# Staging rooms, a deferred store, earlier differences and a last product by token rows in a gated mix of linear attention and eight experts

## The chip, the cores and the metric

The kernel runs on one core of one Trainium2 chip. The metric is the device time of one execution in microseconds (us), lower is better. A core has four compute engines that are used here: TensorE (PE in the profile, with its weight loads as PEld), VectorE (DVE), ScalarE (ACT) and GpSimd (POOL). SyncE (SP) only issues DMAs. Each engine runs its own instructions in the order in which they were written; semaphores hold an instruction until what it needs is there. The kernel schedules by hand: the order on each engine is the order in which the Python program calls the operations, and the tile framework adds the waits.

## What is computed

For 2048 tokens of width 512:

```python
x = A_x
g = sigmoid((x * gate_w).sum(-1, keepdims=True))
a = linear_attention(x, wqkv) @ wo        # 32 heads, phi(t) = (t + 1 if t > 0 else exp(t)) + 1e-6
# mixture: K = 8 of 8 experts, so each token passes all of them
w = softmax(x @ w_gate)
b = sum(w[:, e:e+1] * (silu(x @ w1[e]) @ w2[e]) for e in range(8))   # 512 -> 1792 -> 512
out = g * a + (1 - g) * b
```

Nearly all of the arithmetic is the experts' two matrix products. All of it is in float32; each float32 operand is split into a high and a low part, and a product is three matmuls (high by high, high by low, low by high, `mm3`, L57 to L60).

## The kernel before

**Stages.** `keys` (L319) computes keys and values of the attention and the gates' logits. `experts` (L578) then runs one long loop over steps u. In every step there is a piece of an up product (x by w1) and, from step 58 on, a piece of a down product (hidden by w2), called tick n = u - 58. Both products use a seven-product scheme for 2 by 2 blocks (products P1, P7, P2, P4, P6, P5, P3 in this order): sums and differences of blocks are formed on VectorE, and seven products replace eight. The hidden blocks' differences are formed by `difference` (L716), called by `differ` (L727) at fixed numbers of ticks after a part's first product: kind 1, 2 and 3 at 6, 15 and 29 ticks.

**Groups and steps.** A group g is a pair of hidden blocks of one part (one expert for one half of the tokens); it takes seven steps, k = 0 to 6, one product of 6 matmuls of 512 columns each. Groups 0 and 1 are the attention's queries, groups 2 to 8 are the first expert's. In each step `up` (L644) calls, in order: `other()` (the preparation of the next group's weights, the splits of hidden blocks into high and low by `high`, L741, on ScalarE and `low_h`, L758, on VectorE, and the differences), then the up product, then `mid()` (the tick), then the copies out of PSUM. At k = 6 the last of them is the addition at L696 on VectorE, and the product of the next k = 1 accumulates on the same bank, so it waits for that addition.

**Weights.** For the first half of the tokens, the second weight matrix of an expert is also prepared here: `prep` (L190) makes its high parts on ScalarE (`high2`, L212) and its low parts on VectorE (`low2`, L216) in a staging tile, from which `stash` (L184) stores it to a scratch in device memory, by DMAs of SP's queue. Later `load_w2` (L776) brings these back in pairs, in the order of the ticks. The staging tile number i (0 to 3 in each group) is taken by `ws_tile` (L208): i = 0 is used at k = 1 and stored at k = 2, i = 1 is used at k = 1 and stored at k = 3, i = 2 is used at k = 5 and stored at k = 6, i = 3 is used at k = 6 and stored at the next k = 0. Where it lies is set by `m.spare` (L1112): before step 50 tiles 0 to 2 are taken from `ho` (5 buffers), in the steps 50 to 56 from `xs` (2 buffers), and tile 3 always, and after step 56 all tiles, from `ws` (2 buffers). A buffer can be written again when the DMAs that read it have landed. For the first six pairs of the first expert, the P1 piece is not staged: it is made in the room in which the ticks 0 to 5 use it (`first_w2`, L765) and is stored to the scratch as well, at k = 2 of its group (L250).

**The end.** The last part is the attention's output product for the second half of the tokens, with two pairs: 14 ticks, two for each product. Its results are added by `evict` (L818) to the accumulated sums of the experts in SBUF, which lie with output columns on the partitions; `rows` (L1048) and `columns` (L1056) turn them by TensorE transposes, 128 by 128, copy them out of PSUM and store them. The product P3 is added to the sums of the first 256 columns of the last 512 tokens; after it come the transposes of these sums, the copies and the last stores.

**The start.** SP loads x by four DMAs of 512 columns each, ScalarE's queue loads the first weights by four (L397 to L399). ScalarE makes the high part of x, VectorE makes that of the first weight piece, and the first real matmuls (L451) run. Before them nine matmuls on a tile of zeros run (L513 to L515); that tile is cleared by GpSimd (L388).

Of the kernel before, what the change touches and what calls it, by code (L numbers as in the profile page):

```python
# [16 lines left out]
P = 128  # L17
# [121 lines left out]
def weights(m):  # L139
# [2 lines left out]
    m.ORDER = ("P1", "P7", "P2", "P4", "P6", "P5", "P3")  # L142
    raw, ops, ws = {}, {}, {}
    m.ops = ops
    m.spare = None


    def raw_tile(name, dt=F32):
# [41 lines left out]
    def prep(g, step):  # L190
# [15 lines left out]


        def ws_tile(n):  # L208
            w = ws[g, n] = m.spare(f"wx{g}_{n}") if m.spare and n < 3 else o_tile(f"ws{g}_{n}", "ws", 2, D)
            return w  # L210

        def high2(n, src):  # L212
# [19 lines left out]
        if step == 0:  # L232
            ops[g] = [None] * 7
            high(0, r[:, 0, :, 0], (0, 0), (2, HALF))
        elif step == 1:
            low(0, r[:, 0, :, 0])
            o = o_tile(f"o{g}_1", "oh", 2, HALF)
            act_copy(o[:, 0], r[:, 1, 1, 0])
            ops[g][6] = o, 0
            if both and not begin:  # L240
                ws_tile(0)
            if both:
                act_copy(first(0), r[:, 0, 0, 1])
            high2(1, r[:, :, 1, 1] if both else None)
        elif step == 2:
            o = ops[g][6][0]
            v.tensor_sub(o[:, 1], r[:, 1, 1, 0], f32(o[:, 0]))
            if both:
                v.tensor_sub(first(1), r[:, 0, 0, 1], f32(first(0)))
                stash(part, q, "P1", m.first_w2(q) if begin else ws.pop((g, 0))[:, :, :HALF])  # L250
        elif step == 3:
            low2(1, r[:, :, 1, 1] if both else None, "P2", "P4")
            v.tensor_add(block(1, 1), block(1, 0), block(1, 1))
        elif step == 4:
            v.tensor_sub(block(1, 0), block(0, 0), block(1, 0))
            v.tensor_sub(block(0, 0), block(1, 1), block(0, 0))
        elif step == 5:
            high(2, r[:, 1, :, 0], (5, 0), (1, HALF))
            high2(2, r[:, :, 0, 1] if both else None)
            v.tensor_sub(block(0, 1), block(0, 1), block(0, 0))  # L260
        elif step == 6:
            low(5, r[:, 1, :, 0])
            low2(2, r[:, :, 0, 1] if both else None, "P6", "P7")
            high(3, r[:, 0, :, 0], (3, 0), (4, HALF))
            high2(3, r[:, :, 1, 1] if both else None)
        else:
            low(3, r[:, 0, :, 0])
            low2(3, r[:, :, 1, 1] if both else None, "P3", "P5")
# [44 lines left out]
            low(3, r[:, :, 1], "P3", "P5")  # L313

    m.raw_tile, m.load, m.prep, m.load_wp, m.prep_wp = raw_tile, load, prep, load_wp, prep_wp

def keys(m):  # L319
# [68 lines left out]
    nc.gpsimd.memset(f32(zero), 0.0)  # L388


    gw = [att.tile([P, 2048 + 96 * i], F32R, name=f"g{i}")[:, :2 * KT * G[i]] for i in range(2)]
# [2 lines left out]
    x0 = raw[0] = four(room("x0"))  # L394
    r0 = four(m.raw_tile("r0")[:, :KT * G[0]])
    r1 = [hl_tile(f"r1{i}", F32) for i in range(2)]
    for k in range(KT):  # L397
        nc.sync.dma_start(x0[:, k, :], m.xT[0][:, k * TB:(k + 1) * TB])
        nc.scalar.dma_start(r0[:, k, :], m.wk[:, k * G[0]:(k + 1) * G[0]])  # L399
    for i in range(2):  # L400
        at = KT * G[0] + 2 * i * G[1]
        nc.sync.dma_start(r1[i][:, :, :G[1]], m.wk[:, at:at + 2 * G[1]].rearrange("p (k f) -> p k f", k=2))
    x_tiles(0, 0), x_tiles(0, 1)
    for k in range(KT):
        act_copy(xk(0, 0, k), x0[:, k, :])
# [172 lines left out]
def experts(m, misc):  # L578
# [148 lines left out]
    def differ(u):  # L727
        if u % 7 == 1 and 7 < u < NU + 7 and groups[u // 7 - 1][0].e < E:
            t12, t22 = (raw[u // 7 - 1, f, 1] for f in range(2))
            v.tensor_sub(t12, t22, t12)  # L730
        for pairs, offs in ((NPAIR, (None, 6, 15, 29)), (2, (-3, -1, 1, 5))):
            for kind, off in enumerate(offs):
                if off is None or not 0 <= u - LAG - off < END:
                    continue
                part, prod, q = place(u - LAG - off)
                if part.n == pairs and prod == "P1":
                    difference(kind, part, q)

    SRC = {"P1": 0, "P7": 1, "P2": 2, "P4": 2, "P6": 0, "P5": 0, "P3": 3}
# [78 lines left out]
    def evict(part, prod, sub):  # L818
        b = pb[bank_of(part, prod), sub]
        e = f"{part.h}_{part.e}{sub}"  # L820
        if part is m.A[1]:

            if prod == "P1":
                pb["s", sub] = ps_tile(f"s{sub}", "bc"[sub])
                act_copy(pb["s", sub], b)
                return
            r, j = {"P7": (1, 1), "P2": (0, 0), "P4": (1, 0), "P6": (1, 0), "P5": (1, 1), "P3": (0, 1)}[prod]
            s = sums[1, r * 2 + sub, j]
            for c in range(2) if (prod, sub) == ("P3", 1) else (slice(None),):
# [21 lines left out]

    def tick(n):
        part, prod, k = place(n)
        first = prod in ("P1", "P7")
        for q, sub in STEPS[part.n][k]:
            i = n - k + q
            if q == 0 and first:
                pb[BANK[prod], sub] = ps_tile(f"p{n}_{sub}", "dn")
            w = w2s[i // 2][:, i % 2]
            ds = slice(sub * P, (sub + 1) * P)  # L860
            h = hop[i]
            assert not isinstance(h, tuple)
# [190 lines left out]
        nc.sync.dma_start(m.out[(NHT + i) * P:(NHT + i + 1) * P, :], r)  # L1053


    def columns(dt, tag):  # L1056
        ps = ps_tile(f"oc{dt}", tag)
        for tt in range(NTT):
            nc.tensor.matmul(ps[:, tt * P:(tt + 1) * P], sums[1, dt, 1][:, tt * P:(tt + 1) * P], m.ident,
                             start=tt == 0, stop=True, is_transpose=True, skip_group_check=True)  # L1060
        r = r_tile(f"oc{dt}")
        at = (NHT + NTT) * P
        rows = m.out[at:at + TB, dt * P:(dt + 1) * P].rearrange("(t p) d -> p t d", p=P)
        if dt != 1:
            act_copy(r, ps)
            nc.sync.dma_start(rows, r.rearrange("p (t d) -> p t d", d=P))
            return
        for i, (copy, queue) in enumerate(((act_copy, nc.scalar), (v.tensor_copy, nc.sync))):
            c = slice(i * HALF, (i + 1) * HALF)
            copy(r[:, c], ps[:, c])  # L1070
            queue.dma_start(rows[:, 2 * i:2 * i + 2], r[:, c].rearrange("p (t d) -> p t d", d=P))


    AHEAD = {}
# [21 lines left out]
    for u in range(LAG + NTICK):  # L1096
# [134 lines left out]
```

## Time and profile before

| | |
|---|---|
| median of 3 runs | 2350.26 us (2349.44 to 2350.53) |
| the profiled execution, its own time | 2350.77 us |
| its span (first to last instruction) | 2349.1 us |
| time outside the span in that execution | 1.7 us |
| VectorE busy | 1811.9 us (77%) |
| ScalarE busy | 1419.3 us (60%) |
| GpSimd busy | 158.7 us (7%) |
| DMA | 513.23 MB, mean 218 GB/s |

How to read the profile's rows: a row of the timeline has the start in us from the start of the span, the duration in us, the engine, the line of the kernel, the operation, the names of output and inputs, the shapes and the count, and in brackets how long the engine had been idle and what ended that. "SPq" and "ACTq" are the DMA issues of SyncE and ScalarE. A matmul's duration reaches to the modelled end of its pipeline, so that matmuls that follow one another overlap: their pace is the distance of their starts. A row of the waits has who waited for whom, the total in us, how many times, and the longest. A row of the windows has the stretch, its length, the busy time of PE, PEld, DVE, ACT and POOL with the counts, the granted clock of TensorE, the DMA engines' share and GB/s.

### The profile page before, as it was taken

Reading aid. Unit: us, or ns where it says so; the run is one execution under the profiler, and the core shown is the slowest. Engines: PE = TensorE matmul, PEld = TensorE weight load, DVE = VectorE, ACT = ScalarE, POOL = GpSimd, SP = SyncE. Lnnn points to the kernel's source line nnn. Section 1 sums busy time; section 2 is a strip of 40 time slices with the busy share of each in tenths; the row PEclk is TensorE's granted clock in tenths of the full one; section 3 lists DMA queues with packets and bytes.
Section 4 is the critical chain, followed back from the end, with each engine's and each line's share of the span. In section 5 each row is a group of like instructions: output and inputs, shape, how many; then the busy total and the mean of one; then the engine's idle time right before and its main releaser. Section 6 shows DMA issues by size and latency. Waiting matters only on the chain.

```text
span 2349.1 us, 31301 instructions
## 1 busy us (share of the span) xinstructions
PE 2338.4 (100%) x10492; PEld 1935.4 (82%) x10492; DVE 1811.9 (77%) x3102; ACT 1419.3 (60%) x2655; POOL 158.7 (7%) x222
## 2 busy tenths in 40 slices
PE   9999999999999999999999999999999999999999
PEld 8877888888888888888888888888888888888887
DVE  6798888888888888888677768776676777766666
ACT  6686666666666656666555555555565655555553
POOL 2101000000000000000000000000011000000101
PEclk9999999999999999999999999999999999999999
DMA  7898888988889898988845455654556655555566
GB/s 225 239 311 249 264 288 249 278 263 267 268 267 275 256 290 252 271 269 262 287 144 170 152 172 153 182 186 144 163 166 188 182 150 174 162 166 166 165 220 207
DMA packets 299345, 513.23 MB, mean 218 GB/s; under 512 B 24352, under 2 KB 193840, under 8 KB 298800
## 3 DMA queue, kind: packets, MB, share of 16 engines
q1 hardware_dynamic: 274992, 464.10, 59.8%
q0 software_dynamic: 23344, 46.49, 10.8%
q8 instruction: 82, 1.34, 0.2%
q10 hardware_dynamic: 848, 0.66, 0.1%
q14 instruction: 79, 0.65, 0.1%
HBM read 343.43 MB, written 163.52 MB: 216 GB/s over the span
## 4 chain that ended last, share of the span: by engine, by line
PE 97%; DVE 1%; DMA 1%; issue 0%; ACT 0%; POOL 0%; DVEq 0%; ACTq 0%; POOLq 0%
PE p L58 16%; PE p L60 16%; PE p L59 16%; PE a L58 8%; PE a L60 8%; PE a L59 8%; PE c L59 4%; PE c L58 4%; PE c L60 4%; PE b L60 2%; PE b L59 2%; PE b L58 2%; PE g L451 2%; DMA w2stash<-w 1%; PE y L58 1%; PE y L60 1%
## 5 line engine op out<-in xcount | busy, mean ns | idle before, releaser
L58 PE MATMUL p<-ho,w 128*128 128x512 f32 x1620 | 631.4, 390 | 0.8 <-DVE d L844 0.6
L60 PE MATMUL p<-ho,w 128*128 128x512 f32 x1620 | 630.3, 389 | 0.0
L59 PE MATMUL p<-ho,w 128*128 128x512 f32 x1620 | 630.3, 389 | 0.0
L760 DVE TENSOR_TENSOR ho<-s,ho 128x512 fp32r<-128x512 f32 x784 | 537.2, 686 | 71.2 <-ACT ho L63 67.6
L63 ACT ACTIVATE ho<-s 128x512 fp32r<-128x512 f32 x784 | 487.3, 623 | 21.0 <-PE p L60 8.5
L58 PEld LDWEIGHTS p<-ho,w 128*128 128x128 f32 x1620 | 304.0, 188 | 66.7 <-ACT p L63 1.8
L60 PEld LDWEIGHTS p<-ho,w 128*128 128x128 f32 x1620 | 304.2, 188 | 63.2
L59 PEld LDWEIGHTS p<-ho,w 128*128 128x128 f32 x1620 | 304.1, 188 | 63.0
L63 ACT ACTIVATE o<-rs 128x512 fp32r<-128x512 f32 x224 | 129.1, 576 | 172.7 <-PE a L60 111.7
L690 DVE TENSOR_TENSOR s<-c,s 128x512 f32<-128x512 f32 x116 | 80.2, 692 | 188.6 <-PE c L60 178.7
L63 ACT ACTIVATE o<-rm 128x512 fp32r<-128x512 f32 x240 | 137.5, 573 | 99.8 <-PE a L60 77.4
L63 ACT ACTIVATE s<-a 128x512 f32<-128x512 f32 x116 | 69.5, 599 | 146.9 <-PE a L60 140.3
L63 ACT ACTIVATE ws<-rm 128x512 fp32r<-128x512 f32 x203 | 114.7, 573 | 66.2 <-DMA w2stash<-ws 59.3
L619 ACT ACTIVATE s<-s 128x512 f32<-128x512 f32 x224 | 138.7, 619 | 9.9 <-DVE s L696 6.6
L619 ACT ACTIVATE s<-b 128x512 f32<-128x512 f32 x112 | 67.2, 600 | 112.4 <-PE b L60 100.3
L205 DVE TENSOR_TENSOR o<-rm,o 128x512 fp32r<-128x512 f32 x180 | 122.9, 683 | 0.1
L205 DVE TENSOR_TENSOR o<-rs,o 128x512 fp32r<-128x512 f32 x168 | 114.5, 681 | 0.6 <-ACT o L63 0.6
L219 DVE TENSOR_TENSOR ws<-rm,ws 128x512 fp32r<-128x512 f32 x154 | 105.5, 685 | 0.5 <-ACT ws L63 0.5
L696 DVE TENSOR_TENSOR s<-a,s 128x512 f32<-128x512 f32 x116 | 80.0, 689 | 32.8 <-PE a L60 32.5
L63 ACT ACTIVATE b<-a 128x512 f32<-128x512 f32 x116 | 67.1, 579 | 58.1 <-PE a L60 58.0
L63 ACT ACTIVATE s<-c 128x512 f32<-128x512 f32 x116 | 69.0, 595 | 25.6 <-PE c L60 25.6
L815 POOL DMA_DIRECT2D acct<-c x30 | 25.6, 854 | 794.8 <-DVE c L809 779.8
(321 smaller groups left out, 4540.5 us busy)
## 6 DMA issues: line engine op xcount, KB each, us to landing
w<-w2stash SPq DMA_DIRECT2D x403, 512.0 KB, 4.0
w2stash<-ws SPq DMA_DIRECT2D x357, 256.0 KB, 4.2
rm<-wm SPq DMA_DIRECT2D x228, 256.0 KB, 5.2
rs<-wm SPq DMA_DIRECT2D x108, 256.0 KB, 4.0
wb<-wgtd SPq DMA_DIRECT2D x16, 512.0 KB, 5.2
acct<-c POOLq DMA_DIRECT2D x30, 256.0 KB, 5.6
acct<-d POOLq DMA_DIRECT2D x30, 256.0 KB, 5.5
acct<-k POOLq DMA_DIRECT2D x30, 256.0 KB, 5.5
```

The lines of the kernel that those rows point to most:

```text
L58: nc.tensor.matmul(ps, wh, xh, start=start, stop=False, skip_group_check=True)
L59: nc.tensor.matmul(ps, wh, xl, start=False, stop=False, skip_group_check=True)
L60: nc.tensor.matmul(ps, wlo, xh, start=False, stop=stop, skip_group_check=True)
L63: nc.scalar.activation(dst, src, AF.Copy, scale=scale, bias=bias)
L205: v.tensor_sub(two(o, 1), src, f32(two(o, 0)))
L219: v.tensor_sub(two(w, 1), src, f32(two(w, 0)))
L451: nc.tensor.matmul(ps, xk((0, 0, 1)[j], tb, k, tt * P, (tt + 1) * P), gw[g][:, (0, 1, 0)[j], k, :], start=(k == 0 and j == 0), stop=(k == ...
L619: nc.scalar.activation(dst, src, AF.Silu)
L690: v.tensor_add(sn[g, 2], bank[g, "c"], sn[g, 2])
L696: v.tensor_add(sn[g, 3], bank[g, "a"], sn[g, 3])
L760: v.tensor_sub(h[1], s, f32(h[0]))
L815: nc.gpsimd.dma_start(m.acct[part.h, j, dt], s, accum_op=ALU.add)
```

## The change

1. **Store later** (L250, main loop). The P1 pieces of the first six pairs are no longer stored at k = 2 of their groups (steps 9 to 44) but in pairs at ticks -2, 0 and 2, at the end of the steps 56, 58 and 60.
2. **Staging rooms in turn** (`ws_tile`, `m.spare`). In the steps 50 to 56 only the tiles 0 and 2 come from `xs`; tile 1 comes from `ws`, as tile 3 does.
3. **Differences sooner** (`differ`). For the last expert's part for the second half of the tokens, kinds 2 and 3 are formed 12 and 25 ticks after the first product instead of 15 and 29.
4. **Last product in rows of tokens** (`evict`, `tick`, `turn_last`, `last_rows`, `columns`). P5 is now added to the sums to which P3 was added as well (P3's bank had held its sum too). These sums are turned before P3, into two PSUM banks with tokens on the partitions, and P3 is accumulated on top: for each 128 tokens the hidden block is the stationary operand and the weights move, in matmuls of 256 columns, 24 instead of 12. VectorE copies the first three blocks of tokens out, ScalarE and VectorE half of the fourth each. The sums of the other 256 columns are turned between the two ticks of P3.
5. **Start.** The first x load and its high part are halved, and VectorE instead of GpSimd clears the tile of zeros.

```diff
@@ weights
-    m.spare = None
+    m.spare = lambda n, name: None
...
-            w = ws[g, n] = m.spare(f"wx{g}_{n}") if m.spare and n < 3 else o_tile(f"ws{g}_{n}", "ws", 2, D)
+            w = ws[g, n] = m.spare(n, f"wx{g}_{n}") or o_tile(f"ws{g}_{n}", "ws", 2, D)
...
-                stash(part, q, "P1", m.first_w2(q) if begin else ws.pop((g, 0))[:, :, :HALF])
+                if not begin:
+                    stash(part, q, "P1", ws.pop((g, 0))[:, :, :HALF])
@@ keys
-    nc.gpsimd.memset(f32(zero), 0.0)
+    v.memset(f32(zero), 0.0)
...
+    def pieces(k):
+        return ((0, HALF), (HALF, TB)) if k == 0 else ((0, TB),)
+
     for k in range(KT):
-        nc.sync.dma_start(x0[:, k, :], m.xT[0][:, k * TB:(k + 1) * TB])
+        for lo, hi in pieces(k):
+            nc.sync.dma_start(x0[:, k, lo:hi], m.xT[0][:, k * TB + lo:k * TB + hi])
...
-        act_copy(xk(0, 0, k), x0[:, k, :])
+        for lo, hi in pieces(k):
+            act_copy(xk(0, 0, k, lo, hi), x0[:, k, lo:hi])
@@ experts, differ
-        for pairs, offs in ((NPAIR, (None, 6, 15, 29)), (2, (-3, -1, 1, 5))):
+        for which, offs in (("few", (-3, -1, 1, 5)), ("many", (None, 6, 15, 29)), ("last", (None, 6, 12, 25))):
...
-                if part.n == pairs and prod == "P1":
+                if which == ("few" if part.n == 2 else "last" if part is m.parts[-2] else "many") and prod == "P1":
                     difference(kind, part, q)
@@ experts, evict (last part)
-            r, j = {"P7": (1, 1), "P2": (0, 0), "P4": (1, 0), "P6": (1, 0), "P5": (1, 1), "P3": (0, 1)}[prod]
-            s = sums[1, r * 2 + sub, j]
-            for c in range(2) if (prod, sub) == ("P3", 1) else (slice(None),):
-                c = slice(c * HALF, (c + 1) * HALF) if isinstance(c, int) else c
-                v.tensor_add(s[:, c], b[:, c], s[:, c])
+            for r, j in {"P7": [(1, 1)], "P2": [(0, 0)], "P4": [(1, 0)], "P6": [(1, 0)], "P5": [(0, 1), (1, 1)]}[prod]:
+                s = sums[1, r * 2 + sub, j]
+                v.tensor_add(s, b, s)
@@ experts, tick
+        if part is m.A[1] and prod == "P3":
+            last_rows(n - k, k)
+            return
@@ experts, the end
+    def turn_last():
+        for i in range(2):
+            LR[i] = ps_tile(f"lr{i}", "bc"[i])
+        for dt in range(2):
+            for tt in range(NTT):
+                at = tt % 2 * HALF + dt * P
+                nc.tensor.matmul(LR[tt // 2][:, at:at + P], sums[1, dt, 1][:, tt * P:(tt + 1) * P], m.ident,
+                                 start=dt == 0 and tt % 2 == 0, stop=True, is_transpose=True, skip_group_check=True)
+
+    def last_rows(n, k):
+        ps = LR[k]
+        for t in range(2):
+            tt = 2 * k + t
+            c = slice(t * HALF, (t + 1) * HALF)
+            for q in range(2):
+                w, h = w2s[(n + q) // 2][:, (n + q) % 2], hop[n + q]
+                ts = slice(tt * P, (tt + 1) * P)
+                mm3(ps[:, c], h[0][:, ts], h[1][:, ts], w[:, 0], w[:, 1], False, q == 1)
+            at = (NHT + NTT + tt) * P
+            if tt < NTT - 1:
+                r = r_tile(f"lr{tt}")[:, :HALF]
+                v.tensor_copy(r, ps[:, c])
+                nc.sync.dma_start(m.out[at:at + P, :HALF], r)
+                continue
+            for i, (copy, queue) in enumerate(((act_copy, nc.scalar), (v.tensor_copy, nc.sync))):
+                r = r_tile(f"lr{tt}{i}")[:, :P]
+                copy(r, ps[:, c][:, i * P:(i + 1) * P])
+                queue.dma_start(m.out[at:at + P, i * P:(i + 1) * P], r)
@@ experts, main loop
-        m.spare = ho_tile if u < LAG - 8 else xs_tile if u < LAG - 1 else None
+        def spare(i, name):
+            if u < LAG - 8 and i < 3:
+                return ho_tile(name)
+            if LAG - 8 <= u < LAG - 1 and i % 2 == 0:
+                return xs_tile(name)
...
+        if n in (-2, 0, 2):
+            for q in (n + 2, n + 3):
+                m.stash(m.parts[0], q, "P1", first_w2(q))
...
+        if at == 11:
+            turn_last()
         if at == 12:
             for dt in (2, 3):
-                columns(dt, "bc"[dt - 2])
-    for dt in range(2):
-        columns(dt, "dn")
+                columns(dt)
```

In this numbering LAG is 58, HALF is 256, TB is 512, NTT is 4 and `at` counts ticks from the start of the last part. `columns` now always copies by ScalarE in one piece and stores by SP.

More of the change, by code (lines that the diff above doesn't have):

```diff
@@ L315, in weights @@
     m.raw_tile, m.load, m.prep, m.load_wp, m.prep_wp = raw_tile, load, prep, load_wp, prep_wp
+    m.stash = stash
 def keys(m):
@@ L1053, in rows, with columns @@
         nc.sync.dma_start(m.out[(NHT + i) * P:(NHT + i + 1) * P, :], r)
-    def columns(dt, tag):
-        ps = ps_tile(f"oc{dt}", tag)
+    def columns(dt):
+        ps = ps_tile(f"oc{dt}", "dn")
         for tt in range(NTT):
@@ L1061, in columns @@
         r = r_tile(f"oc{dt}")
+        act_copy(r, ps)
         at = (NHT + NTT) * P
[L1063 to L1071, printed above, removed]
+        nc.sync.dma_start(m.out[at:at + TB, dt * P:(dt + 1) * P].rearrange("(t p) d -> p t d", p=P),
+                          r.rearrange("p (t d) -> p t d", d=P))
+    LR = {}
+    def turn_last():
[25 more added lines that the diff above has]
+                queue.dma_start(m.out[at:at + P, i * P:(i + 1) * P], r)
     AHEAD = {}
@@ L1110, in mid @@
                 rows_first(g - ROWS0, k)
-        m.spare = ho_tile if u < LAG - 8 else xs_tile if u < LAG - 1 else None
+        def spare(i, name):
[3 more added lines that the diff above has]
+                return xs_tile(name)
+        m.spare = spare
         def other():
```

## The prediction

> **What bounds the kernel now.** I read the page first, then TensorE's waits, then the windows and the timeline around each wait.
>
> ```profile
> PE 2338.4 (100%) x10492; PEld 1935.4 (82%) x10492; DVE 1811.9 (77%) x3102; ACT 1419.3 (60%) x2655; POOL 158.7 (7%) x222
> w<-w2stash SPq DMA_DIRECT2D x403, 512.0 KB, 4.0
> ```
>
> TensorE is busy for 2338.4 of 2349.1 us. The change removes no matmul columns, so only the 10.7 us in which TensorE stands still, and stretches in which it is slow, can be won. TensorE's own waits tell where:
>
> ```profile
> PE a L58 <- DVE s L696: 3.9, 2, 3.2
> PE p L58 <- DVE d L844: 0.6, 1, 0.6
> ```
>
> The other idle time is the first 1.45 us and the end after the last matmul. The large wait (3.2 us) lies here; the windows, and TensorE alone in the timeline:
>
> ```profile
> 120.00:140.00 20.00, 19.23 (x82) 14.97 (x81) 17.97 (x31) 17.99 (x34) 2.29 (x5) 1.00 0.93 314
> 180.00:190.00 10.00, 6.85 (x26) 5.27 (x25) 6.79 (x11) 5.91 (x12) 0.00 (x0) 0.90 0.66 216
> ```
> ```profile
> 135.79 0.50 PE L58 MATMUL a<-t6h,o 128*128 128x512 f32 x1 [0.70 <-DVE s L696]
> ```
> ```profile
> 179.98 0.39 PE L59 MATMUL a<-t3l,o 128*128 128x512 f32 x1
> ...
> 184.28 0.39 PE L60 MATMUL a<-x00h,o 128*128 128x512 f32 x1
> ...
> 187.82 0.70 PE L58 MATMUL a<-t6h,o 128*128 128x512 f32 x1 [3.15 <-DVE s L696]
> ...
> 191.58 0.40 PE L58 MATMUL c<-t1h,o 128*128 128x512 f32 x1
> ```
>
> From 179.98 to 184.28 there are 19 matmul steps, 0.226 us each. From 184.28 to 191.58 there are 10, in 7.30 us instead of 2.26: 5.04 us are lost. Of these 3.31 are the wait (187.82 - 184.28 - 0.23); the other 1.73 come after it, while the granted clock is low (0.90 in that window). The wait of 0.70 us at 135.79 left the clock at 1.00. Now who was late:
>
> ```profile
> 179.19 8.28 SPq L186 DMA_DIRECT2D w2stash<-wx  x5
> ...
> 182.05 0.69 DVE L690 TENSOR_TENSOR s<-c,s 128x512 f32<-128x512 f32 x1 [0.64 <-PE c L60]
> 182.66 0.68 DVE L205 TENSOR_TENSOR o<-rm,o 128x512 fp32r<-128x512 f32 x1
> 185.21 0.63 ACT L63 ACTIVATE wx<-rm 128x512 fp32r<-128x512 f32 x1 [3.46 <-DMA w2stash<-wx]
> ...
> 187.08 0.69 DVE L696 TENSOR_TENSOR s<-a,s 128x512 f32<-128x512 f32 x1
> ...
> 189.00 1.81 SPq L186 DMA_DIRECT2D w2stash<-ws  x2
> ...
> 193.35 0.63 ACT L63 ACTIVATE ws<-rm 128x512 fp32r<-128x512 f32 x1 [1.93 <-DMA rm<-wm]
> ```
>
> This is step 54 to 57, group 8. Tiles 0, 1 and 2 want the two `xs` buffers, so tile 2 (ScalarE, 185.21) waits until the store of tile 0, issued at 179.19, has landed. VectorE stands in order behind it: low part of tile 2, a hidden split, and only then L696, for which TensorE waits.
>
> **The rooms in turn.** With tile 1 in `ws`, tile 2 takes the second `xs` buffer, and nobody has used it: ScalarE's 3.46 us go. The two `ws` buffers are then asked for by tile 1 at step 50, whose buffer was last stored at step 42, and by tile 3 at step 55, stored at step 49, seven products or about 9.5 us of matmuls before, against 4 to 6 us to land. What is late next is VectorE itself. From L690 at 182.05 four operations stand in front of L696's end at the measured distance of 0.61: L205, the low part of tile 2, the hidden split (new in this group, since the ticks come near), then L696 with 0.69. So L696 ends at 182.05 + 4 x 0.61 - 0.03 + 0.69 = 185.15, TensorE resumes at 185.2 instead of 184.51. A wait of 0.7 remains, and 0.11 for the slower first matmul after it (0.50 against 0.39 in the row at 135.79). A wait of that length left the clock alone before, so I count the clock's loss as gone. Gain 5.04 - 0.81 = **4.2 us**. Bounds: 5.0 if the rest wait vanishes; about 2.5 if the clock falls all the same.
>
> Here a rule of the Trainium skill can be weighed, page "TensorE: Matmul & The Clock Gate", section "Why this matters for your kernels": no idle gaps of TensorE over about 3 us, since one window of idle time puts the clock back to half. The 3.15 us above with the fall after it agrees; 0.7 is far below, so by the rule as by the row the 1.73 us come back.
>
> **The second wait of ScalarE** (1.93 at 193.35, tile 1 of group 9 behind tile 3 of group 8 in `ws`) stays: its store is issued one VectorE chain after L696 as before. Behind it on ScalarE stand a hidden split and the copies of step 57 and 58; TensorE needs the last of them in step 61, four steps on. I cost it at nothing, for its distance from TensorE's restart is as before (193.35 - 187.82 = 5.5 us); without that cover it would be 1 to 3 us.
>
> **The stores later.** Six DMAs leave SP's queue at steps 9 to 44 and come back at steps 56, 58 and 60, two each, behind the loads of the next weights and ahead of the first loads from the scratch. 256 KB each, 1.5 MB in all, into a stretch in which 256 KB stores take 4 us to land. The rooms are read again only after ticks 1, 3 and 5, and the first load from the scratch is needed five ticks after it is issued; a step is now 12 matmuls, 2.7 us, so 13 us of cover against 4.0 (page row). I cost it at nothing; the earlier stretch gains slack but TensorE does not wait there.
>
> **Differences sooner.** Two places of the last expert, VectorE and TensorE:
>
> ```profile
> 2281.48 0.69 DVE L723 TENSOR_TENSOR s<-s,s 128x512 f32<-128x512 f32 x1
> ...
> 2281.65 0.50 PE L58 MATMUL p<-ho,w 128*128 128x512 f32 x1
> ...
> 2283.46 0.50 PE L58 MATMUL p<-ho,w 128*128 128x512 f32 x1
> ```
> ```profile
> 2302.05 0.68 DVE L725 TENSOR_TENSOR s<-s,s 128x512 f32<-128x512 f32 x1
> ...
> 2302.41 0.39 PE L60 MATMUL p<-ho,w 128*128 128x512 f32 x1
> 2302.65 0.68 DVE L844 TENSOR_TENSOR d<-p,d 128x512 f32<-128x512 f32 x1
> ...
> 2303.39 0.50 PE L58 MATMUL p<-ho,w 128*128 128x512 f32 x1 [0.60 <-DVE d L844]
> ```
>
> L844 empties the bank that TensorE wants at 2302.41 + 0.23 = 2302.64 and gets at 2303.39. Ahead of it stands L725, a difference of kind 3, which now runs four ticks sooner. L844 then starts at 2302.05, TensorE at 2302.79: 0.60 won. At 2281.48 a difference of kind 2 stands ahead of the copy that frees the other bank; the tick should have begun at 2281.65 + 0.34 + 5 x 0.23 = 2283.14 and began at 2283.46; with the 0.6 of L723 gone the wait goes, with the slow restart 0.4. The moved differences land where VectorE has idle time. Sum **1.0 us**, bounds 0.5 and 1.1.
>
> **The end.**
>
> ```profile
> 2338.79 1.04 PE L1022 MATMUL o<-ident,tl 128*128 128x128 f32 x8
> ...
> 2339.58 0.47 PE L58 MATMUL p<-ho,w 128*128 128x512 f32 x1
> ...
> 2343.07 0.39 PE L60 MATMUL p<-ho,w 128*128 128x512 f32 x1
> ...
> 2344.78 0.38 ACT L63 ACTIVATE oc<-oc 128x256 f32<-128x256 f32 x1 [0.25 <-PE oc L1059]
> ...
> 2345.20 0.42 DVE L1070 COPY oc<-oc 128x256 f32<-128x256 f32 x1 [0.94 <-ACT oc L63]
> 2345.65 0.37 SPq L1071 DMA_DIRECT2D y<-oc  x1
> ```
> ```profile
> y<-o SPq DMA_DIRECT2D x4, 256.0 KB, 2.1
> ...
> y<-oc SPq DMA_DIRECT2D x1, 128.0 KB, 2.5
> ```
> ```profile
> 7.59 1.12 PE L451 MATMUL g<-g,x00h 128*128 128x256 f32 x8
> ...
> 8.55 0.64 PE L451 MATMUL g<-g,x00l 128*128 128x256 f32 x4
> ```
>
> Eight transposes take 0.79 (2338.79 to 2339.58); a matmul of 256 columns takes (8.55 - 7.59) / 8 = 0.12 and ends 0.28 after its start (0.64 - 3 x 0.12). The row at 2345.20 shows what matters: VectorE waited 0.94, until ScalarE had done its copy from the same PSUM bank, though the columns differ. The changed kernel's instruction order has the same guard between TensorE and VectorE: the first matmul of the second 128 tokens of each bank waits for the copy of the first 128. So, after the same 2339.58: eight transposes, 2340.37; six matmuls with 0.09 for the change of kind, the last ending at 2341.34; copy 0.42 with 0.04 and 0.06 around it, TensorE again at 2341.86 instead of 2341.18; six more, 2342.69; eight transposes, 2343.48; six, ending 2344.44; copy, 2344.96; six, ending 2345.95. ScalarE's copy of 128 columns (0.38 less the slope, about 0.27) ends at 2346.26, VectorE's, one after the other, at 2346.6, where the last store is issued: 0.96 later than now. That store has 64 KB and little in front of it, the present one 128 KB behind 384 KB: it lands in 2.0 to 2.1 instead of 2.5 (256 KB alone take 2.1). Net **0.5 us lost**, bounds 0 and 1.0.
>
> By the Trainium skill, page "PSUM — Partial Sum Buffer", section "PSUM bank collisions raise a hardware error", two engines are kept apart by bank and partitions, not by address; the row at 2345.20 agrees. Were the guard by address, the two copies would hide and the end would be 1.4 us sooner.
>
> **The start.** The rows:
>
> ```profile
> 0.87 0.53 POOL L388 MEMSET zero<- 128x512 f32 x1
> ...
> 1.45 4.21 PE L515 MATMUL idle<-zero 128*128 128x512 f32 x9 [1.45 <-POOL ones L423]
> ...
> 4.47 0.63 ACT L63 ACTIVATE x00h<-x 128x512 fp32r<-128x512 f32 x1 [0.47 <-DMA x<-xT]
> ...
> 5.46 1.82 PE L451 MATMUL g<-g,x00h 128*128 128x256 f32 x8
> ```
>
> No VectorE memset is in the trace; between 0.30 (a cast of 256 columns, nearest in kind) and 0.69 I take GpSimd's 0.53, no gain. Half an x copy takes 0.38 instead of 0.63, so the first matmul can begin up to 0.25 sooner, but the nine on zeros end about then. One more load makes nine at once, and in the changed order the last x load waits for the first weights to land, over 2 us later than now, about 3 us before TensorE wants it. I take **0.15 us** gained, bounds -0.5 and 0.5.
>
> **Sum.** 4.2 + 1.0 + 0.15 - 0.5 = 4.85 us, 2350.77 - 4.85 = 2345.9 by the profiled execution, which lies 0.5 above the median; by the median 2345.4 us.
>
> **Rivals.** (a) The rest wait at step 57 and the copies at the end cost less than worked out: gain 5.8, 2344.5 us. For it: L696 is only 0.7 late; against: its chain is in the instruction order. (b) The wait moves: ScalarE waits longer for a `ws` buffer at step 57, because the six late stores crowd the queue, and TensorE waits in step 61 for 1 to 3 us: gain 2.9, 2347.4. For it: the DMA share is 0.93 just before; against: the page of rows has 0.66 at 180 to 190. (c) The rooms do not come free either, tile 1 or 3 waits as tile 2 did: gain 0.65, 2349.6. Against: 9.5 us against 4 to 6. (d) The clock falls in the last 7 us, where transposes and waits leave 36 short stretches of matmuls: the last 24 matmuls at double pace, 24 x 0.12 = 2.9 lost, gain 2.0, 2348.3. The clock page's part on transposes says that they do not count as busy in the Trainium skill ("TensorE: Matmul & The Clock Gate", section "Part 4: PE-mode transpose"); no run here shows it yet. (e) Slower: the late stores delay the first three loads from the scratch beyond their ticks. It decides when a load takes over 13 us instead of 4.0. Each such wait priced like the one at 187.82, 5.0: 15 - 4.85 = 10 us slower, 2360.
>
> **How the numbers follow.** Chances: forecast 0.52, (a) 0.18, (b) 0.15, (c) 0.05, (d) 0.05, (e) 0.05. 0.2% is 4.7 us, about what a measurement of this kernel can tell from no change. The forecast lies just beyond that; two thirds of it I count as faster: 0.34 + 0.18 = 0.52. Within: 0.18 + 0.25 = 0.43. Slower 0.05. The range leaves out (c), (d) and (e) and thin ends: gains of 2.4 to 6.4, 2343.9 to 2347.9.
>
> **What would show it.** Right: no ScalarE wait of 3 us on a stored tile near 182; L696 ends near 185.15, TensorE waits 0.5 to 0.9 there, clock 1.00 after it; no wait on L844 near 2300; two waits of some 0.6 on VectorE copies inside the last product, and the last store issued about 1 us later after the last turning of rows. Wrong: TensorE waits on the scratch or on ScalarE between 186 and 205, or a clock below 1.00 after 190.

## The result, and the profile after

The changed kernel takes 2346.38 us in the median of 22 runs (2345.39 to 2348.94), the kernel before 2349.99 in the median of 22 (2347.99 to 2351.20). The ratio is 0.9986, 95% interval 0.9980 to 0.9992: some 3.6 us, or 0.15%, faster; 2345.4 was forecast, in a range of 2343.9 to 2347.9. The profiled execution of the changed kernel took 2345.67 us, its span is 2344.0, so this pair of profiles lies 5.1 us apart. Lines below L250 are moved: L690 is now L698, L696 is L704, L760 is L768, L844 is L851, L1022 is L1032, L1059 is L1069.

TensorE's waits of the changed kernel:

```profile
PE idle L523 <- DVE zero L390: 1.5, 1, 1.5
PE a L58 <- DVE s L704: 1.2, 2, 0.7
PE lr L58 <- DVE lr L1101: 1.0, 2, 0.5
PE g L459 <- ACT g L63: 0.2, 1, 0.2
```

The 3.2 us on the addition at k = 6 are 0.7 at most, the wait on L844 is gone, and two waits of 0.5 on VectorE's copies of the last product are new. The windows around the old wait, with PE, PEld, DVE, ACT and POOL busy, the granted clock, the DMA share and GB/s:

```profile
120.00:140.00 20.00, 19.26 (x83) 14.99 (x82) 17.92 (x32) 17.86 (x34) 2.29 (x5) 1.00 0.90 295
180.00:190.00 10.00, 9.46 (x43) 7.49 (x42) 8.39 (x15) 7.00 (x14) 0.00 (x0) 1.00 0.86 275
190.00:200.00 10.00, 10.00 (x46) 8.29 (x45) 8.67 (x18) 7.11 (x14) 0.00 (x0) 1.00 0.99 315
```

From 180 to 190 TensorE does 43 matmuls instead of 26, and the clock stays at 1.00. The timeline of the same place, all engines:

```profile
181.28 0.62 ACT L63 ACTIVATE wx<-rm 128x512 fp32r<-128x512 f32 x1
...
181.70 0.69 DVE L698 TENSOR_TENSOR s<-c,s 128x512 f32<-128x512 f32 x1 [0.65 <-PE c L60]
...
183.92 0.39 PE L60 MATMUL a<-x00h,o 128*128 128x512 f32 x1
184.11 0.68 DVE L704 TENSOR_TENSOR s<-a,s 128x512 f32<-128x512 f32 x1
...
184.85 0.50 PE L58 MATMUL a<-t6h,o 128*128 128x512 f32 x1 [0.54 <-DVE s L704]
...
187.02 0.39 PE L58 MATMUL c<-t1h,o 128*128 128x512 f32 x1
...
190.01 0.63 ACT L63 ACTIVATE ws<-rm 128x512 fp32r<-128x512 f32 x1 [2.74 <-DMA w2stash<-ws]
```

ScalarE's copy of tile 2 waits for no store any more. L704 ends 3.09 us after the start of L698 (184.79 - 181.70); 3.10 were forecast. The ten matmul steps from 183.92 to 187.02 lose 3.10 - 2.26 = 0.84 instead of 5.04; 0.81 was forecast. ScalarE's second wait is there, 2.74 us, and TensorE runs through it: the window from 190 is full.

The matmul behind the short wait, the differences and the end, from the timeline of the changed kernel:

```profile
135.41 0.50 PE L58 MATMUL a<-t6h,o 128*128 128x512 f32 x1 [0.69 <-DVE s L704]
...
2276.83 0.50 PE L58 MATMUL p<-ho,w 128*128 128x512 f32 x1
...
2278.33 0.39 PE L58 MATMUL p<-ho,w 128*128 128x512 f32 x1
...
2297.19 0.39 PE L60 MATMUL p<-ho,w 128*128 128x512 f32 x1
2297.57 0.50 PE L58 MATMUL p<-ho,w 128*128 128x512 f32 x1
```
```profile
2332.90 1.03 PE L1032 MATMUL o<-ident,tl 128*128 128x128 f32 x8
...
2336.03 0.39 PE L58 MATMUL lr<-w,ho 128*128 128x256 f32 x1 [0.52 <-DVE lr L1101]
...
2339.12 0.39 PE L58 MATMUL lr<-w,ho 128*128 128x256 f32 x1 [0.52 <-DVE lr L1101]
...
2340.13 0.28 ACT L63 ACTIVATE lr<-lr 128x128 f32<-128x128 f32 x1 [1.56 <-PE lr L60]
2340.44 0.29 DVE L1106 COPY lr<-lr 128x128 f32<-128x128 f32 x1 [1.38 <-ACT lr L63]
2340.47 0.36 ACTq L1107 DMA_DIRECT2D y<-lr  x1
2340.76 0.34 SPq L1107 DMA_DIRECT2D y<-lr  x1
```

Before, the bank near 2302 came 0.75 late (2303.39 against 2302.64); now 0.15 (2297.57 - 2297.19 - 0.23). From the last turning of rows to the last store's issue it is 7.86 (2332.90 to 2340.76), before 6.86. The same points in the two profiles, before less after, tell where the 5.1 us lie: the matmul after the short wait 135.79 - 135.41 = 0.38; the tick 2281.65 - 2276.83 = 4.82; the last turning 2338.79 - 2332.90 = 5.89; the last issue 2345.65 - 2340.76 = 4.89; the end 5.1. So 0.38 lie ahead of the short wait, 4.44 in the middle and 1.07 at the differences, and the end took 0.8. The 0.38 can't be given to the change: two profiles of the kernel before differ by 0.82 at that point (below). Of the 4.44, 4.20 are the rooms (5.04 - 0.84); the other 0.2 is lost at two late starts of matmuls near 1150 and 1159 in this profile of before, which the second profile of before doesn't have.

### The profile page after: what moved, and what is told of

It is laid out like the page before. It is cut to its first block, busy times and chain, and to the rows that moved or that the text cites. A ratio compares the mean times of both kernels' runs of the same rounds, so it can differ in the third digit from the quotient of the medians.

```text
span 2344.0 us, 31327 instructions
## 1 busy us (share of the span) xinstructions
PE 2336.0 (100%) x10504; PEld 1934.3 (83%) x10504; DVE 1813.5 (77%) x3105; ACT 1417.3 (60%) x2655; POOL 158.9 (7%) x221
## 4 chain that ended last, share of the span: by engine, by line
PE 99%; ACT 0%; DVE 0%; issue 0%; DMA 0%; SPq 0%; ACTq 0%
PE p L58 16%; PE p L60 16%; PE p L59 16%; PE a L58 9%; PE a L60 9%; PE a L59 9%; PE c L60 4%; PE c L58 4%; PE c L59 4%; PE b L60 2%; PE b L58 2%; PE b L59 2%; PE g L459 2%; PE y L58 1%; PE y L60 1%; PE y L59 1%
## 5 line engine op out<-in xcount | busy, mean ns | idle before, releaser
L768 DVE TENSOR_TENSOR ho<-s,ho 128x512 fp32r<-128x512 f32 x784 | 537.1, 686 | 70.0 <-ACT ho L63 66.4
L698 DVE TENSOR_TENSOR s<-c,s 128x512 f32<-128x512 f32 x116 | 80.2, 691 | 186.0 <-PE c L60 176.1
L63 ACT ACTIVATE ws<-rm 128x256 fp32r<-128x256 f32 (+1 forms) x204 | 115.7, 573 | 81.4 <-DMA w2stash<-ws 72.6
L704 DVE TENSOR_TENSOR s<-a,s 128x512 f32<-128x512 f32 x116 | 80.0, 690 | 33.0 <-PE a L60 32.3
```

Source lines behind the costliest of these rows:

```text
L63: nc.scalar.activation(dst, src, AF.Copy, scale=scale, bias=bias)
L698: v.tensor_add(sn[g, 2], bank[g, "c"], sn[g, 2])
L704: v.tensor_add(sn[g, 3], bank[g, "a"], sn[g, 3])
L768: v.tensor_sub(h[1], s, f32(h[0]))
```

## The experiments

Twelve runs were made, in three groups, each beside the kernel before, whose median was 2350.06, 2350.30 and 2350.14 us in them. Among the twelve are the kernel before and the changed kernel once more, and one kernel twice. My theory was the one on record: the wait belongs to the staging room, and it brings 4.2 of the 4.85 us. The main rivals were that the later stores do it, and that single profiles mislead.

**Rooms alone** (part 2 of the change on the kernel before):
```diff
-            w = ws[g, n] = m.spare(f"wx{g}_{n}") if m.spare and n < 3 else o_tile(f"ws{g}_{n}", "ws", 2, D)
+            w = ws[g, n] = m.spare(n, f"wx{g}_{n}") or o_tile(f"ws{g}_{n}", "ws", 2, D)
...
-        m.spare = ho_tile if u < LAG - 8 else xs_tile if u < LAG - 1 else None
+        def spare(i, name):
+            if u < LAG - 8 and i < 3:
+                return ho_tile(name)
+            if LAG - 8 <= u < LAG - 1 and i % 2 == 0:
+                return xs_tile(name)
+
+        m.spare = spare
```


> The kernel before with the staging rooms in turn alone; the P1 stores stay where they were. Theory (the room of tile 2 is the cause): ScalarE's wait of 3.5 us near 182 is gone, TensorE waits 0.5 to 0.8 us at its place near 184.6 instead of 3.15, the clock stays at 1.00 there, and the profiled span is 4.2 to 4.5 us shorter than 2349.1. Rival (the crowded queue is the cause, and the six stores must leave it too): a wait of over 1.5 us for a stored tile stays on ScalarE between 182 and 186, and TensorE waits over 1.5 us.

2346.08 us (2345.56 to 2346.65), ratio 0.9984, interval 0.9975 to 0.9993. TensorE's waits of this kernel:

```profile
PE a L58 <- DVE s L696: 1.2, 2, 0.7
PE p L58 <- DVE d L844: 0.6, 1, 0.6
```

The long wait is gone with the stores left where they were, and ScalarE waits for no store between 178 and 190: the room is the cause, worth 4.0 us in the medians and 4.7 in the profiled spans (2344.4 against 2349.1; 4.2 to 4.5 expected). This kernel is as fast as the one with all five parts, which took 2346.38 and, in another group, 2346.10: the other four parts together bring nothing that the medians show.

**Later stores alone.**
```diff
-                stash(part, q, "P1", m.first_w2(q) if begin else ws.pop((g, 0))[:, :, :HALF])
+                if not begin:
+                    stash(part, q, "P1", ws.pop((g, 0))[:, :, :HALF])
...
+        if n in (-2, 0, 2):
+            for q in (n + 2, n + 3):
+                m.stash(m.parts[0], q, "P1", first_w2(q))
```


> The kernel before with the later P1 stores alone; tiles 0, 1 and 2 still share the two xs buffers. Theory (room): ScalarE still waits for the store of tile 0, which is issued near 179 and takes 4 us or more, so 1.5 to 3 us remain and TensorE waits 1.5 to 3 us near 185; gain 0 to 2 us, with the clock's loss in it. Rival (queue): the store lands so early that TensorE waits 0.8 us or less, and the gain is 4 us, as with the rooms.

2350.04 us, ratio 1.0000 (0.9992 to 1.0009). Of TensorE's waits the one that counts, and ScalarE's behind it:

```profile
PE a L58 <- DVE s L698: 3.3, 2, 2.6
```
```profile
183.99 0.63 ACT L63 ACTIVATE wx<-rm 128x512 fp32r<-128x512 f32 x1 [2.96 <-DMA w2stash<-wx]
```

TensorE waits 2.6 instead of 3.2, ScalarE 2.96 for the stored tile instead of 3.46, and the time doesn't change. TensorE waits for no load from the scratch, so the slower rival (e) has no place either.

**Last product in rows alone** (part 4 of the change on the kernel before):
```diff
+        if part is m.A[1] and prod == "P3":
+            last_rows(n - k, k)
+            return
```


> The kernel before with the last product in rows of tokens alone. Theory (one bank, two engines): two waits of about 0.5 us of TensorE on VectorE's copies inside the last product, the last store issued 1.0 us later after the last turning of rows, span 0.5 to 1.0 us longer. Rival (fewer steps behind the last matmul pay): span shorter by 0.5 us or more.

2352.11 us (2349.61 to 2352.64), ratio 1.0008 (0.9999 to 1.0017). Its waits have the two new ones:

```profile
PE lr L58 <- DVE lr L1093: 1.0, 2, 0.5
```

From the last turning to the last issue it is 7.86 again. The median is 2.0 above that of before, more than the 0.5 forecast, though the interval just reaches no loss. Its one run at a mean clock of 1.000 took 2349.61, its others 2352.1 in the median; against the like runs of before (2348.31 and 2350.39, below) that is 1.3 and 1.7. Of this 0.3 lies outside the span (2.0 against 1.7).

**The kernel before, once more.** No edit.

> The kernel before itself, to see its own spread. Theory (the clock falls after the 3.15 us wait only in some executions, since the wait is hardly as long as what makes it fall): the times lie in two heaps about 1.7 us apart, those with a granted clock of 0.999 high and those with 1.000 low. Rival (the spread has another source): the clock is the same in both heaps, or there are no heaps.

2350.07 us, ratio 0.9999 (0.9990 to 1.0008), but its profiled execution took only 2348.12, with the same wait of 3.2 us. The reason stands in windows cut at the clock's own steps: TensorE's clock changes in the records only at distances of whole multiples of 3.413 us from the moment at which it is first full (7.045 us in the first profile of before, 4.60 in this one). The first profile of before, cut so:

```profile
181.12:184.54 3.42, 3.42 (x16) 2.62 (x14) 1.58 (x3) 0.63 (x2) 0.00 (x0) 1.00 1.01 353
184.54:187.95 3.41, 0.26 (x2) 0.13 (x2) 2.08 (x4) 2.74 (x6) 0.00 (x0) 1.00 0.25 85
187.95:191.36 3.41, 3.41 (x9) 2.63 (x10) 3.41 (x7) 3.20 (x7) 0.00 (x0) 0.50 0.58 193
191.36:194.77 3.41, 3.41 (x17) 2.81 (x16) 0.93 (x4) 1.48 (x4) 0.00 (x0) 1.00 0.89 183
```

And this one:

```profile
182.09:185.51 3.42, 1.69 (x8) 1.07 (x6) 0.85 (x2) 1.17 (x3) 0.00 (x0) 1.00 0.58 205
185.51:188.92 3.41, 1.97 (x9) 1.62 (x10) 3.41 (x7) 3.41 (x7) 0.00 (x0) 1.00 0.49 159
188.92:192.33 3.41, 3.41 (x17) 2.83 (x16) 2.26 (x5) 1.35 (x4) 0.00 (x0) 1.00 0.80 193
```

Column three is TensorE's busy time, the third from the end the granted clock. In the first the wait fills one stretch (0.26 busy of 3.41), and the next is granted half; here the same wait lies across a border (1.69 and 1.97 busy), and the clock stays. The rows agree in three more profiles with a long wait: 0.91 and 0.74 busy in one stretch, in the kernels with the later stores alone and with the differences alone, and half the clock after it; with the last product alone 1.96 and 1.84, and no fall. So it took more than 1.7 us of idle time and no more than 2.5 within one stretch. Of 98 runs of before in the three groups, 77 have a mean granted clock under 1.000 and a median of 2350.39; the other 21 have 2348.31. The mark is not exact, since a fall behind the last matmul counts a little in the mean too, but the times part at it: none of the 77 is below 2349.38, none of the 21 above. One stretch of 3.413 us at half the clock can cost at most 1.71, near the 1.73 that I had, so the fall doesn't account for all of the 2.1 us between the medians. The start may hold the rest; that is not shown for the runs without a profile. In this profile the matmul behind the short wait came 0.82 sooner than in the first one (135.79), with the clock first full at 4.60 instead of 7.05:

```profile
134.97 0.50 PE L58 MATMUL a<-t6h,o 128*128 128x512 f32 x1 [0.69 <-DVE s L696]
```

The Trainium skill, page "TensorE: Matmul & The Clock Gate", section "What's actually happening", says that activity is judged in a window of 3413 ns that runs on its own and doesn't start with the kernel. These windows agree: their borders lie 3.413 us apart, and where they lie differs from one execution to the next. The limit that the same page of the Trainium skill gives for gaps, about 3 us (section "Why this matters for your kernels"), is too simple by them: 3.18 us of idle time left the clock alone, 2.65 us did not.

**Differences alone.**
```diff
-        for pairs, offs in ((NPAIR, (None, 6, 15, 29)), (2, (-3, -1, 1, 5))):
+        for which, offs in (("few", (-3, -1, 1, 5)), ("many", (None, 6, 15, 29)), ("last", (None, 6, 12, 25))):
```


> The kernel before with the last expert's differences of kinds 2 and 3 sooner (12 and 25 ticks instead of 15 and 29) and nothing else. The theory: the wait of 0.60 on the emptied bank near 2302 goes and the tick near 2283 begins 0.4 sooner, so 1.0 us less in the trace between the first matmul of the rooms' stretch and the last rows; the median 2349.0 against 2350.0. Rival: the moved differences push another VectorE operation late at the new places, TensorE waits there, and the median does not move.

2348.65 us, ratio 0.9993 (0.9984 to 1.0002): 1.5 below its before in the medians, 1.0 expected, no proof by itself. (All its 11 runs have a mean clock under 1.000; against the like runs of before, 2350.39, it is 1.7.) The waits are clearer; all that this kernel has are these two:

```profile
PE a L58 <- DVE s L696: 3.4, 2, 2.8
PE idle L515 <- POOL ones L423: 1.4, 1, 1.4
```

L844 is gone from them, and nothing took its place.

**The change without its last product** (the old end):

> The changed kernel with the last product as it was before. From the turning of the last two rows to the end of the span the kernels with the old tail took 10.3 us, those with the new one 11.1 and 11.3. Theory (the new tail costs time): 0.7 to 1.0 us faster than the changed kernel, median 2345.4 to 2345.7. Rival (the tail is even): 2346.2 to 2346.6.

2346.20 us, ratio 0.9984 (0.9976 to 0.9993): the theory fails, the rival's time came. The last store is issued 6.87 after the last turning instead of 7.86, but of this 1.0 the median shows nothing. What the earlier issue gave was used up behind it: the span ended 3.73 after the last issue, against 3.20 in the changed kernel, and 2.0 us lay outside the span, against 1.7. With the halved first load and the last product both old or both new it was 1.7 in each profile; with only one of them new 2.0 or 2.1, in four profiles. Why, no run shows.

**The change with the whole first load** and GpSimd's clearing:

> The changed kernel with the first load whole and the zeros cleared by GpSimd, as before. Theory (the new start gains nothing, since the nine loads in flight and the pairing of copies delay the next pieces as much as the first one comes sooner): median within 0.3 us of the changed kernel, rather below it, 2346.0 to 2346.4. Rival (the start gains 0.2 to 0.4 us): 2346.6 to 2346.8.

2346.99 us, ratio 0.9987 (0.9978 to 0.9996): 0.6 above the changed kernel's median of the first group, 0.9 above that of the last one, so not the theory's time and somewhat more than the rival's. Its start is compared below.

**Token blocks with the banks in turn.** The two waits of 0.5 came, I held, because each bank takes two neighbouring blocks, so the second block's matmuls wait for the first one's copy. With the blocks in the order 0, 2, 1, 3 a copy runs beside matmuls into the other bank:
```diff
-        ps = LR[k]
         for t in range(2):
-            tt = 2 * k + t
-            c = slice(t * HALF, (t + 1) * HALF)
+            tt = 2 * t + k
+            ps = LR[t]
+            c = slice(k * HALF, (k + 1) * HALF)
```


> The changed kernel with the four blocks of 128 tokens in the order 0, 2, 1, 3, so that two blocks that follow one another lie in different PSUM banks; no other edit. Theory (the bank's guard holds TensorE): both waits on VectorE's copies in the last product go, the last store is issued 1.2 to 1.4 us sooner after the last turning of rows, median about 2345.1. Rival (VectorE's copies or SP's issues were the limit in any case): the waits go, the end moves by less than 0.4 us.

2345.48 us (2344.88 to 2346.13), ratio 0.9980 (0.9971 to 0.9989). Its timeline at the place:

```profile
2336.83 0.28 PE L59 MATMUL lr<-w,ho 128*128 128x256 f32 x1
2336.91 0.42 DVE L1101 COPY lr<-lr 128x256 f32<-128x256 f32 x1 [1.17 <-PE lr L60]
2336.95 0.28 PE L60 MATMUL lr<-w,ho 128*128 128x256 f32 x1
```

TensorE goes on at its pace of 0.12 while VectorE copies; the issue comes 6.30 after the last turning, 1.56 sooner. Of these 0.6 go again at the last store, which lands in 2.6 instead of 2.0. In the medians the kernel is 0.6 to 0.9 below the changed one (2346.10 and 2346.38, in other groups), where 1.3 was expected.

**And one hidden split later.** The rest wait of 0.54 hangs on VectorE's four operations in a row. One of them, the low part of a hidden block (L768), is wanted only ticks later and can be left to the next step:
```diff
-            while lows < min(n + 4, highs, END):
+            while u != LAG - 3 and lows < min(n + 4, highs, END):
```


> As banks_in_turn, and the first hidden split's low part is made one step later, so that it no longer stands in front of the addition for which TensorE waits near 185. Theory (VectorE's order is what is left of that wait): TensorE's 0.54 us near 184.85 fall to 0.1 or less, median 0.5 to 0.6 us below that of banks_in_turn, about 2344.5. Rival (something else holds the addition): the wait stays at 0.4 us or more.

2345.00 us, ratio 0.9978 (0.9969 to 0.9986): 0.5 below the banks in turn, as expected, though their runs overlap. Of the waits on that line only the one near 135 is left:

```profile
PE a L58 <- DVE s L704: 0.7, 1, 0.7
```

**This version, with the two starts, beside the changed kernel.** One group of three:

> The changed kernel with the token blocks of the last product in the order 0, 2, 1, 3, the low part of tile 2 of the group at step 57 put behind that step, and the first load whole with GpSimd's memset of the zeros, as before the change. If the halved first load costs what the traces show (the second piece of x is copied at 6.0 to 7.0 us instead of 5.4 to 5.6, and the first matmul of the rooms' stretch starts 0.6 us later), this kernel ends about 0.6 us sooner than the one beside it with the halved load: 2344.4 us. Rival: the start's difference is chance from one execution to the next, and the two medians agree within 0.3 us. Forecast of the prediction: the halved load gains 0.15, so this one 0.15 later.

> The same kernel with the halved first load and VectorE's memset of the zeros, as in the changed kernel. It gave 2345.0 us before, so 2345.0 again; beside the kernel with the whole first load it is 0.6 us slower by the traces, 0.15 faster by the prediction, and equal by the rival of chance. Against the changed kernel: the copies' two waits (2 x 0.5, with the slow restarts 1.6) and the wait of 0.54 at step 57 are gone, so 1.4 us faster.

> The changed kernel itself beside the other three, as their yardstick: 2346.4 us again. By the theory its last product costs 1.0 us (two waits on the copies), and the rest wait at step 57 stays 0.5 to 0.7; by the rival that these are details of one profiled execution, one or both of them are absent in this profile.

(The text on record of the first calls the moved operation the low part of tile 2; it is the hidden split, as VectorE's rows in the kernel with the halved load show. The low part of the tile, at 183.41, stays ahead of L704.)

```profile
182.21 0.69 DVE L698 TENSOR_TENSOR s<-c,s 128x512 f32<-128x512 f32 x1 [0.63 <-PE c L60]
182.81 0.68 DVE L205 TENSOR_TENSOR o<-rm,o 128x512 fp32r<-128x512 f32 x1
183.41 0.68 DVE L219 TENSOR_TENSOR wx<-rm,wx 128x512 fp32r<-128x512 f32 x1
184.02 0.68 DVE L704 TENSOR_TENSOR s<-a,s 128x512 f32<-128x512 f32 x1
184.62 0.68 DVE L205 TENSOR_TENSOR o<-rm,o 128x512 fp32r<-128x512 f32 x1
```

Whole first load: 2345.28 us (2344.44 to 2345.64), ratio 0.9980 (0.9971 to 0.9989). Halved: 2344.81 (2344.13 to 2345.56), ratio 0.9978 (0.9969 to 0.9987). The changed kernel: 2346.10 (2345.59 to 2346.71), ratio 0.9983 (0.9974 to 0.9992). The halved load's kernel is 0.5 faster by the medians, not 0.6 slower, as the traces had made me expect; the rival of equal times (within 0.3) doesn't fit well either. The best version's runs all lie below the changed kernel's in this group: 1.3 us by the medians, 1.4 expected. The changed kernel's second profile has the same two waits on L704 (1.2 in all) and the same two on the copies (1.0), so they are no chance of one execution.

## Why the prediction was right, point by point, and where not

**The rooms: right, in mechanism and size.** 0.84 us are left of 5.04, 0.81 was forecast, and the kernel with the rooms alone gains 4.0 in the medians, 4.2 forecast. The chain of four VectorE operations came out to 0.01. The cover that I gave the `ws` buffer of tile 3 was miscounted: from step 49 to 55 there are six products, 6 x 6 x 0.226 = 8.1 us, not seven; no wait appeared on it.

**The clock: right in direction, but not in every execution.** I took the 1.73 from the one profile as a fixed price of a 3.15 us wait. By the mean clock it is paid in 77 of 98 runs; that costs the median little, since most runs of before pay it. The profiled pair (5.1) says more than the medians (3.6 to 4.0), because the profile of before lies 0.8 above its median and that of the changed kernel 0.7 below. The step "which lies 0.5 above the median; by the median 2345.4" failed: it put all of the offset on the old kernel and took the new one to sit at its median. By the profile's own time the sum said 2345.9, and 2345.67 came. That this is so near is in part luck: 0.38 of the pair's difference lies in the start, where 0.15 was forecast for another reason and two executions of one kernel differ by 0.82.

**The other four parts: 0.65 forecast, nothing measured.** The sum had 1.0 + 0.15 - 0.5 for them. In the medians the whole change (2346.10 and 2346.38) is no faster than the rooms alone (2346.08). The differences' gain shows in the trace, but the end gives back most of it, as the next points tell, and the groups can't settle what is left.

**ScalarE's second wait and the later stores: right, nothing.** The wait of 2.74 us came and TensorE did not see it. Rivals (b), (c) and (e) have no row among the changed kernel's waits (one profile of the banks in turn has 0.2 us on a load from the scratch, at 1146 us, far behind the late stores); nor has (d): the changed kernel's window over the last product has the clock at 1.00.

```profile
2333.00:2340.10 7.10, 6.06 (x49) 5.45 (x47) 2.56 (x5) 2.17 (x4) 0.00 (x0) 1.00 0.62 212
```

**The differences: right.** 1.07 against 1.0: 0.60 at the bank, 0.31 at the tick after 2276.83, which takes 1.50 instead of 1.81 (2281.65 to 2283.46), and 0.11 for the slow restart after it.

**The end: right in its steps, too small in its sum.** The issue comes 1.00 later (0.96 forecast), behind two waits. The landing is as forecast; the page rows of the changed kernel's last stores:

```profile
y<-lr ACTq DMA_DIRECT2D x1, 64.0 KB, 2.1
y<-lr SPq DMA_DIRECT2D x1, 64.0 KB, 2.0
```

But from the landing to the end of the span it is 1.2 now (2344.0 - 2340.76 - 2.0), before 0.9 (2349.1 - 2345.65 - 2.5). I had kept that stretch fixed. So the term is -0.8 in the profiles, not -0.5, and alone on the kernel before -2.0 in the medians. By the Trainium skill, page "PSUM — Partial Sum Buffer", section "PSUM bank collisions raise a hardware error", two engines are kept apart by bank, not by address. The experiment with the banks in turn shows that the guard in this kernel goes by bank: the two waits of 0.52 are gone as soon as the matmuls go to the other one. What the chip would do without the guard, no run shows.

**The start: not as reasoned.** The changed kernel's rows:

```profile
1.00 0.48 DVE L390 MEMSET zero<- 128x512 f32 x1 [1.00 <-PEq L1270]
...
4.01 0.42 ACT L63 ACTIVATE x00h<-x 128x256 fp32r<-128x256 f32 x1
...
4.75 0.42 ACT L63 ACTIVATE x00h<-x 128x256 fp32r<-128x256 f32 x1 [0.33 <-DMA x<-xT]
...
5.22 1.11 PE L459 MATMUL g<-g,x00h 128*128 128x256 f32 x8
...
6.01 0.63 ACT L63 ACTIVATE x00h<-x 128x512 fp32r<-128x512 f32 x1 [0.84 <-DMA x<-xT]
...
7.00 1.21 PE L459 MATMUL g<-g,x00h 128*128 128x256 f32 x8 [0.19 <-ACT g L63]
```

The first matmul on data came 0.24 sooner in this pair (5.22 against 5.46), but not because of the halved load. It stands behind the nine on zeros, and these end by the clock. In the five profiles with the clock first full by 4.98 (the changed kernel: 4.83) it began at 5.21 to 5.29, in the nine with 5.56 or later (before: 7.05) at 5.45 to 5.54. With the halved load it came up to 0.09 later within each of the two: VectorE's zeros are ready at 1.48 instead of 1.40, and the nine begin at 1.53 instead of 1.45. So of my two clauses "the first matmul can begin up to 0.25 sooner" failed, and "but the nine on zeros end about then" was what counted. A half takes 0.42, not the 0.38 that I took, and the next piece of x comes later: its copy starts at 6.01 here and at 7.04 in the first profile with both later edits, against 5.44 and 5.59 with the whole load. Behind it on ScalarE stands the copy of the next weight piece, for which TensorE waited 0.2, 0.7 and 1.1 us in three of six profiles. The first matmul that accumulates y starts at 17.50 to 18.52 in six profiles with the halved load, at 17.06 to 18.11 in eight with the whole one. So the start itself gained nothing. Still the medians put the halved load 0.5 ahead (2344.81 against 2345.28) and 0.6 to 0.9 in the changed kernel, as forecast in sign (0.15): by the profiles this lies behind the last store, in the landing (2.6 against 2.8) and in the 1.7 against 2.1 us outside the span. What ties the first load to the end stays open, and so does whether 0.5 is more than chance, since the runs overlap.

## What to carry to other kernels

When one engine waits for another, follow the chain back to the buffer: a change of which staging buffer a tile takes removed a 3.15 us wait, without one operation less. A part of a change can be tried alone: here one part of five gave all that the medians show. A single profile prices a wait only as that execution paid it; where the clock may fall, look at where its stretches begin and at the spread of the runs before a difference of two profiles is called a gain. Where the guard goes by bank, as in this kernel, a PSUM bank that is copied out in parts holds back matmuls into its other parts, so let consecutive blocks alternate between two banks.

## What the runs showed of the hardware that was not expected

- The granted clock changes at a raster of 3.413 us whose phase differs from one execution to the next: it was first full at 4.60 to 7.73 us of the span in fourteen profiles, and whether a wait of 3.2 us costs half the clock for one stretch hangs on that phase. It moves the start as well: the first matmul on data began at 5.21 to 5.29 us or at 5.45 to 5.54.
- The last store, 64 KB, landed in 2.0 to 2.4 us in the four profiles with the last product by rows and its first order of blocks, where SP's issue before it began 1.62 us earlier (1.63 in one), and in 2.6 to 2.8 in the four with the banks in turn, where it began 0.84 earlier. That the one makes the other wait is argued, not tried.
- What lies behind the last landing isn't fixed: 0.9 to 1.3 us to the end of the span, and 1.7 or 2.0 to 2.1 us outside it, by the kernel: all runs of one kernel lie within 0.2 us in this.
